# Turned quarters ahead of the scores, attention outputs later, and GpSimd normalising in two more units of a fused attention and gated-MLP kernel

## The chip, the cores and the metric

The kernel runs on one core of one Trainium2 chip. The metric is the device time of one execution in microseconds (us). Engines: PE (TensorE), with PEld for its weight loads, DVE (VectorE), ACT (ScalarE), POOL (GpSimd) and SP (SyncE), which here only issues DMAs.

## What is computed

Attention over 8 batches, 12 heads, 448 positions and 64 dimensions per head, with a softmax whose denominator has one extra term, and then two matrix products with an activation (Mish) between them:

```
scores = (q @ k.T) / sqrt(64)
m      = max(scores, axis=-1)
e      = exp(scores - m)
attn   = e / (sum(e) + exp(-m) + 1e-9)
x      = (attn @ v), heads side by side        # 3584 x 768
h      = x @ w_in                              # 3584 x 2048
out    = (h * tanh(softplus(h))) @ w_out       # 3584 x 768
```

Inputs and output are float32; the kernel's matrix products take bf16.

## The kernel before

Heads are taken in pairs: six pairs a batch, 48 in all, numbered from 0. The scores of a pair need seven tiles of 128 query rows, done in four half steps of two, two, two and one tiles. There are three pairs of score banks (`sc`), used in turn, and two single banks (`mo`) for everything else.

For a half step PE writes the scores, DVE takes the negated row maximum (L270, `negm`), and ACT writes the exponentials with their sums (L283) into one of four buffers `en`, chosen by the pair's number modulo four. So pair 10 overwrites pair 6's buffer and pair 11 overwrites pair 7's. Once a pair is done, its exponentials are multiplied by the reciprocal denominators (`normalise`, L302: seven passes of 128x448, on DVE at L317, or on GpSimd at L315, with a copy of the reciprocals made by DVE at L308), and then turned so that keys lie on partitions (`eT`). Most pairs are turned by a DMA transpose that SP issues (L321). Pairs 5, 6 and 7 (`BY_PE`) are turned by PE instead, a quarter at a time: `turn_on_pe` makes seven transposes into an `mo` bank (L332) and DVE copies the bank out (L336). `av_pair` (L344) multiplies a pair's `eT` with v (L358) and the result is copied into `xT` (L367).

Pairs 0 to 5 are done in a loop of their own. After it the work goes in units of three pairs; unit 2 holds pairs 6 to 8 and unit 3 pairs 9 to 11. A unit has twelve half steps (loop over n, L546), followed by eight blocks of the first matrix product and Mish (loop over f, `mm1_mish`, L375). The product in units 2 and 3 is that of batch 0, so it needs pairs 0 to 5 alone. From unit 4 on the half steps also carry parts of the second matrix product (L446), dealt out by weight.

The order is written by hand. Within a half step it is: the exponentials, the outstanding bank copies (`flush_late`), parts of the second product, the scores of the half step three ahead as far as score banks are free, loads and casts, attention outputs (`AV_AT`), turned quarters, and weight loads (`W_AT`). Each engine runs its instructions in the order in which the program issues them. Casts to bf16 and normalising share GpSimd with the issue of the weight loads (L148). Loads of q, k and v and the DMA transposes share SP's queue.

In the f loop of a unit, its first pair in the order `todo` is normalised at f = 0, the second at f = 3, and the third at f = 4 on GpSimd from unit 4 on, or at f = 7 on DVE in units 2 and 3. `todo` puts pairs turned by PE last: 8, 6, 7 in unit 2 and 9, 10, 11 in unit 3.

Of the kernel before, what the change touches and what calls it, by code (L numbers as in the profile page):

```python
# [15 lines left out]
UNIT_PAIRS = 3  # L16
# [3 lines left out]
def kernel(  # L20
# [15 lines left out]
    NT = 4  # L36
# [5 lines left out]
    UNITS_PER_B = HP // UNIT_PAIRS  # L42
    N_UNITS = B * UNITS_PER_B
    HU = 2 * UNIT_PAIRS
    FF_U = FF_T // UNITS_PER_B
# [3 lines left out]
    STEPS = 4  # L49
# [53 lines left out]
    def flush_late():  # L103
        while late:
            late.popleft()()

    def mo_take():

        if not mo_free:
            flush_late()  # L110
        return mo_free.popleft()
# [183 lines left out]
    def denominators(st):  # L295
        nc.vector.scalar_tensor_tensor(
            out=st["den"], in0=st["sums"], scalar=1e-9, in1=st["expm"],
            op0=ALU.add, op1=ALU.add,
        )
        nc.vector.reciprocal(out=st["rden"], in_=st["den"])  # L300

    def normalise(p, dma=True, on_pool=False):  # L302
        st = att[p]
        en = st["en"]
        if on_pool:

            st["rden2"] = st_pool.tile([128, NTILE], FP32, tag="rden2", name="rden2")
            nc.vector.tensor_copy(out=st["rden2"], in_=st["rden"])  # L308
        for i in range(NTILE):
            args = dict(  # L310
                out=en[:, :, i, 0:SP_], in0=en[:, :, i, 0:SP_],
                scalar1=st["rden2" if on_pool else "rden"][:, i : i + 1],
            )
            if on_pool:
                nc.gpsimd.tensor_scalar(scalar2=1.0, op0=ALU.mult, op1=ALU.mult, **args)  # L315
            else:
                nc.vector.tensor_scalar(scalar2=None, op0=ALU.mult, **args)  # L317
        eT = eT_pool.tile([128, NT, 2 * S], BF16, tag="eT", name="eT")
        st["eT"] = eT
        if dma:  # L320
            nc.sync.dma_start_transpose(  # L321
                out=eT.rearrange("c j (i q) -> c (j i) q", q=128),
                in_=en.rearrange("q j i c -> q (j i c)"),
            )

    def turn_on_pe(p, j, act=False):

        st = att[p]
        own = mo_take()
        ps = own[:, :].bitcast(BF16).rearrange("c (i q) -> c i q", q=128)  # L330
        for i in range(NTILE):
            nc.tensor.transpose(ps[0:SP_, i, :], st["en"][:, j, i, 0:SP_], ident)  # L332
        copy = nc.scalar.copy if act else nc.vector.tensor_copy

        def evac():
            copy(  # L336
                out=st["eT"][0:SP_, j, :].rearrange("c (i q) -> c i q", q=128),
                in_=ps[0:SP_, 0:NTILE, :],
            )
            mo_free.append(own)  # L340

        late.append(evac)
# [74 lines left out]
    def mm2_part(g, i, q0, nq):  # L417

        b0, b1 = 2 * g, 2 * g + 1
        cols, n_cols = slice(q0 * NQ, (q0 + nq) * NQ), nq * NQ  # L420
        st = {}
        if i < 3:
            src, c0 = gT[b0], i * 128
        elif i == 3:
            src, c0 = mids[g], 0
        else:
            src, c0 = gT[b1], i * 128 - S

        def evac():
            if (g, i) not in o_sbs:  # L430
                o_sbs[g, i] = [o_pool.tile([128, d_model], FP32, tag="o_sb", name="o_sb"), 0]
            o_sb, have = o_sbs[g, i]
            nc.vector.tensor_copy(out=o_sb[:, cols], in_=st["o"][:, 0:n_cols])  # L433
            mo_free.append(st["o"])
            o_sbs[g, i][1] = have + nq
            if (g, i) == (B // 2 - 1, 6):
                store_rows(g, i, o_sb, cols)
            elif have + nq == 4:
                store_rows(g, i, o_sb, slice(0, d_model))

        def chunk(f0, f1):
            if f0 == 0:
                flush_late()
                st["o"] = mo_take()
            for ff in range(f0, f1):
                nc.tensor.matmul(  # L446
                    st["o"][:, 0:n_cols],
                    lhsT=src[:, ff, c0 : c0 + 128],
                    rhs=w_out_sb[:, ff, cols],
                    start=(ff == 0), stop=(ff == FF_T - 1),  # L450
                )
            if f1 == FF_T:
                late.append(evac)

        step = 2
        return [(lambda f0=f0: chunk(f0, f0 + step), nq) for f0 in range(0, FF_T, step)]

    steps = UNIT_PAIRS * STEPS
    first_mm2 = 2 * UNITS_PER_B
# [27 lines left out]
    LOAD_AT = (0, 3, 6)  # L487
    HEAD = HP

    BY_PE = {HEAD - 1: 1, HEAD: 0, HEAD + 1: STEPS}  # L490
    AV_AT = {0: {5: 3, 7: 4, 10: 5}, 1: {3: 8, 6: 6, 10: 7}}

    W_AT = ({5: 1, 9: 1}, {1: 1, 5: 1, 7: 1, 9: 1, 11: 1}, {1: 1, 3: 1, 5: 1, 7: 1})
    for p in range(UNIT_PAIRS):
        load_pair(p)
    for p in range(2):
# [35 lines left out]
    denominators(att[HEAD - 1])  # L532
    normalise(HEAD - 1, dma=HEAD - 1 not in BY_PE)

    for u in range(UNITS_PER_B, N_UNITS + 2 * UNITS_PER_B):
        attn = u < N_UNITS
        filler = deque()
        for part in plan.get(u, []):
            filler.extend(mm2_part(*part))
        total, done, acc = sum(w for _, w in filler), 0, 0.0  # L540
        p0 = u * UNIT_PAIRS
        if attn and u >= first_mm2:
            av_with.update({p0 + i: p0 + i - UNIT_PAIRS for i in range(UNIT_PAIRS)})
        end = min((u + 1) * UNIT_PAIRS, N_PAIRS) * STEPS

        for n in range(steps):  # L546
            pi, s = divmod(n, STEPS)
            p, idx = p0 + pi, p0 * STEPS + n
            late_tp = u == UNITS_PER_B and n == STEPS
            if late_tp:  # L550
                transpose_pair(p0 + 2)
            exps(idx)
            if late_tp:
                evac_qk(p0 + 2)
            if u == UNITS_PER_B + 1 and n == 0:
                for j in range(2):
                    turn_on_pe(HEAD, j)
            flush_late()
            acc += weight[n]
            want = int(total * acc / sum(weight) + 1e-6)  # L560
            while done < want:
                fn, w = filler.popleft()
                fn()
                done += w
            scores_ahead(end)
            if n in LOAD_AT:
                load_pair(p0 + LOAD_AT.index(n) + LEAD)
                cast_pair(p0 + LOAD_AT.index(n) + LEAD - 1)
            early = AV_AT.get(u - UNITS_PER_B)
            if early is not None:  # L570
                if n in early:
                    av_pair(early[n])
                for pe, n0 in BY_PE.items():
                    first = 2 if pe == HEAD else 0
                    if pe // UNIT_PAIRS == u - 1 and n0 + first <= n < n0 + NT:
                        turn_on_pe(pe, n - n0)
            elif s == (2 if pi else 0) and N_PAIRS <= p < N_PAIRS + UNIT_PAIRS:
                av_pair(p - UNIT_PAIRS)
            if u - UNITS_PER_B < len(W_AT):
                load_w(W_AT[u - UNITS_PER_B].get(n, 0))  # L580
        assert done == total

        moe = u < N_UNITS + UNITS_PER_B
        b, w = (u - UNITS_PER_B) // UNITS_PER_B, u % UNITS_PER_B
        nxt = p0 + UNIT_PAIRS
        todo = sorted(range(p0, nxt), key=lambda p: p in BY_PE)
        for f in range(FF_U):
            if moe:
                mm1_mish(b, w * FF_U + f)
            if u == UNITS_PER_B and f in (2, 6) or u == UNITS_PER_B + 1 and f == 1:  # L590
                load_w(1)
            if not attn:
                continue
            if f == 0:
                denominators(att[p0]["whole"])
                normalise(todo[0], dma=todo[0] not in BY_PE)
            if f == 3:
                scores_ahead(min(nxt * STEPS + 1, N_PAIRS * STEPS))
            if f in (1, 3, 5):
                transpose_pair(nxt + f // 2, bank=f // 2 % 2)  # L600
                evac_qk(nxt + f // 2)
            if f >= FF_U - 2:
                scores_ahead(min(nxt * STEPS + f - FF_U + 4, N_PAIRS * STEPS))
            if f == 3:
                normalise(todo[1], dma=todo[1] not in BY_PE)
            if f == (4 if u >= first_mm2 else FF_U - 1):
                normalise(todo[2], dma=todo[2] not in BY_PE, on_pool=u >= first_mm2)
        if moe and w == UNITS_PER_B - 1:
            gather_mid(b)
    flush_late()  # L610
# [31 lines left out]
```

## Time and profile before

| | |
|---|---|
| time, median of 3 runs | 493.58 us (492.65 to 493.93) |
| time of the profiled execution | 492.95 us |
| its span | 491.2 us |
| PE busy | 451.8 us (92%) |
| DVE busy | 352.7 us (72%) |
| ACT busy | 349.5 us (71%) |
| POOL busy | 152.1 us (31%) |
| PE's share of the chain that ended last | 74% |

Times in the views are counted in us from the start of the span. A slice is one fortieth of the span, 12.28 us, and its digit the busy share in tenths. `[2.07 <-ACT en L283]` behind an instruction says how long its engine stood idle before it, and what released it. A view of waits gives the total, the number and the longest of the waits of one kind. `x7` says that seven instructions are merged into one row. The rows of a table by stretches have, after the length, the busy time of PE, PEld, DVE, ACT and POOL with the number of instructions, then the granted PE clock (1.00 is full), the mean busy share of the DMA engines, and GB/s.

### The profile page before, as it was taken

How to read it: one execution, taken by the hardware profiler on the slowest of the kernel's cores; microseconds unless marked ns; L12 is line 12 of the kernel's file. 1: busy time of each engine (PE TensorE's matmuls, PEld its weight loads, DVE VectorE, ACT ScalarE, POOL GpSimd, SP SyncE). 2: the span in 40 equal slices, each digit the busy share in tenths (PEclk: the TensorE clock that was granted, in tenths of full speed). 3: DMA queues.
4: the chain of work that ended last, by engine and by line, in shares of the span. 5: the costliest groups of instructions: out<-in, count | busy, mean ns of one | idle time of the engine just before them, and what ended most of it. 6: DMA issues, size and time to landing. Idle time of an engine off the chain costs nothing.

```text
span 491.2 us, 8805 instructions
## 1 busy us (share of the span) xinstructions
PE 451.8 (92%) x2992; PEld 249.3 (51%) x2992; DVE 352.7 (72%) x714; ACT 349.5 (71%) x906; POOL 152.1 (31%) x252
## 2 busy tenths in 40 slices
PE   4466995898999999999999999999999999999996
PEld 2222442454555555555555555556555565556563
DVE  4898987788868787878788786878797878420021
ACT  5988675768788887979697978888797979502300
POOL 4622270701433534252523324253435230300000
PEclk9999998799999999999999999999999999999999
DMA  8999999999999999899999979898999796780112
GB/s 221 207 211 214 245 212 154 239 166 223 190 231 249 215 226 195 240 187 250 147 247 198 216 175 206 209 216 234 176 260 174 170 177 141 132 157 21 45 37 93
DMA packets 209452, 92.19 MB, mean 188 GB/s; under 512 B 166272, under 2 KB 205952, under 8 KB 209408
## 3 DMA queue, kind: packets, MB, share of 16 engines
q1 hardware_dynamic: 201920, 85.35, 81.7%
q0 software_dynamic: 7488, 6.29, 9.1%
q8 instruction: 23, 0.38, 0.3%
q14 instruction: 21, 0.17, 0.1%
HBM read 45.61 MB, written 11.01 MB: 115 GB/s over the span
## 4 chain that ended last, share of the span: by engine, by line
PE 74%; DVE 10%; ACT 7%; DMA 6%; issue 2%; SPq 1%; POOL 0%; DVEq 0%; ACTq 0%
PE mo L446 26%; PE mo L382 24%; PE sc L249 9%; ACT en L283 6%; PE sc L358 6%; DVE negm L270 5%; DMA eT<-en 5%; PE sc L382 3%; DVE en L317 3%; PE sc L179 3%; PE mo L358 1%; DMA k_f<-in_k_dram 1%; DVE xT L367 1%; SPq L121 1%; PE mo L332 0%
## 5 line engine op out<-in xcount | busy, mean ns | idle before, releaser
L283 ACT ACTIVATE en<-sc,negm 128x448 bf16<-128x448 f32 x336 | 209.6, 638 | 31.9 <-DVE negm L270 14.5
L270 DVE TENSOR_REDUCE negm<-sc 128x2 f32<-128x896 f32 x192 | 182.6, 969 | 56.3 <-PE sc L249 44.9
L446 PE MATMUL mo<-w_out_sb,gT 128*128 128x384 bf16 (+1 forms) x896 | 142.1, 303 | 0.0
L382 PE MATMUL mo<-xT,w_in_sb 128*128 128x448 bf16 x672 | 140.3, 352 | 0.4 <-DVE xT L367 0.4
L388 ACT ACTIVATE gT<-mo 128x448 bf16<-128x448 f32 x112 | 59.4, 543 | 72.4 <-PE mo L382 72.2
L446 PEld LDWEIGHTS <-gT 128*128 128x128 bf16 x896 | 84.0, 98 | 46.8 <-issue 1.3
L382 PEld LDWEIGHTS <-w_in_sb 128*128 128x128 bf16 x768 | 72.8, 98 | 64.6 <-issue 3.8
L315 POOL TENSOR_SCALAR en<-en,rden 128x448 bf16<-128x448 bf16 x84 | 52.8, 650 | 93.8 <-DVE rden L308 86.9
L162 POOL CAST q_bf<-q_f 112x512 bf16<-112x512 f32 x47 | 28.9, 616 | 160.2 <-DMA q_f<-in_q_dram 151.1
L249 PE MATMUL sc<-kT,qd 128*128 128x448 bf16 x252 | 71.6, 354 | 1.5 <-DVE qd L210 0.7
L317 DVE TENSOR_SCALAR en<-en,rden 128x448 bf16<-128x448 bf16 x252 | 69.7, 347 | 0.9
L283 ACT ACTIVATION_READ_ACCUMULATOR en<-sc,negm 128x1 f32 x336 | 69.4, 207 | 0.0
L433 DVE COPY o_sb<-mo 128x384 f32<-128x384 f32 (+1 forms) x64 | 32.1, 502 | 41.3 <-PE mo L446 41.2
L249 PEld LDWEIGHTS <-qd 128*128 128x128 bf16 x252 | 23.9, 97 | 31.8 <-issue 13.8
L358 PE MATMUL sc<-eT,v_bf 112*64 112x448 bf16 x288 | 34.1, 357 | 2.0 <-ACT en L283 1.8
L164 POOL CAST v_bf<-v_f 112x512 bf16<-112x512 f32 x48 | 29.6, 616 | 15.4 <-DMA v_f<-in_v_dram 14.1
L255 PE MATMUL sc<-kT,qd 64*128 64x448 bf16 x36 | 17.7, 508 | 17.9 <-ACT en L283 16.1
L358 PEld LDWEIGHTS <-v_bf 112*64 112x64 bf16 x384 | 21.0, 115 | 25.4 <-issue 18.7
L163 POOL CAST k_bf<-k_f 112x512 bf16<-112x512 f32 x47 | 29.0, 617 | 5.1 <-DMA k_f<-in_k_dram 4.0
L210 DVE TENSOR_SCALAR qd<-sc 64x448 bf16<-64x448 bf16 x72 | 27.8, 386 | 0.9
L218 ACT COPY kT<-sc 128x448 bf16<-128x448 bf16 x39 | 20.8, 534 | 7.0 <-PE sc L179 7.0
L446 PE MATMUL mo<-w_out_sb,mid 128*128 128x384 bf16 x128 | 24.9, 326 | 0.0
(50 smaller groups left out, 307.3 us busy)
## 6 DMA issues: line engine op xcount, KB each, us to landing
q_f<-in_q_dram SPq DMA_DIRECT2D x48, 224.0 KB, 5.1
k_f<-in_k_dram SPq DMA_DIRECT2D x48, 224.0 KB, 5.3
v_f<-in_v_dram SPq DMA_DIRECT2D x48, 224.0 KB, 5.5
w_in_sb<-in_moe_w_in_dram POOLq DMA_DIRECT2D x12, 256.0 KB, 5.8
w_out_sb<-in_moe_w_out_dram POOLq DMA_DIRECT2D x8, 384.0 KB, 7.5
out_dram<-o_sb SPq DMA_DIRECT2D x7, 336.0 KB, 3.4
out_dram<-o_sb SPq DMA_DIRECT2D x8, 288.0 KB, 4.5
out_dram<-o_sb SPq DMA_DIRECT2D x8, 240.0 KB, 3.4
```

The costliest lines, as they stand in the source:

```text
L163: cast_k(out=k_bf, in_=k_f.rearrange(by_t, t=NT))
L164: nc.gpsimd.tensor_copy(out=v_bf, in_=v_f)
L249: nc.tensor.matmul(sc[:, bk, 0:S], lhsT=qT[:, i].rearrange("d h r -> d (h r)"), rhs=kT, start=True, stop=True,)
L270: nc.vector.tensor_reduce(out=negm, in_=sc[:, 0 : len(cols), 0:S], axis=AX.X, op=ALU.max, negate=True)
L283: nc.scalar.activation(out=st["en"][:, :, c, 0:SP_], in_=sc[:, bk, 0:S].rearrange("q (j c) -> q j c", j=NT), func=AF.Exp, bias=st["negm"][ ...
L315: nc.gpsimd.tensor_scalar(scalar2=1.0, op0=ALU.mult, op1=ALU.mult, **args)
L317: nc.vector.tensor_scalar(scalar2=None, op0=ALU.mult, **args)
L358: nc.tensor.matmul(av[h * 64 : (h + 1) * 64, 0:S], lhsT=v_bf[:, h, j * D : (j + 1) * D], rhs=e_h, start=(j == 0), stop=(j == NT - 1),)
L382: nc.tensor.matmul(h_ps[:, 0:S], lhsT=w_in_sb[:, dm, ff * 128 : (ff + 1) * 128], rhs=xT[b][:, dm, :], start=(dm == 0), stop=(dm == DM_T - 1),)
L388: nc.scalar.activation(out=gT[b][:, ff, :], in_=h_ps[:, 0:S], func=AF.Mish)
L433: nc.vector.tensor_copy(out=o_sb[:, cols], in_=st["o"][:, 0:n_cols])
L446: nc.tensor.matmul(st["o"][:, 0:n_cols], lhsT=src[:, ff, c0 : c0 + 128], rhs=w_out_sb[:, ff, cols], start=(ff == 0), stop=(ff == FF_T - 1),)
```

## The change

In unit 3 the quarters of pairs 6 and 7 are turned ahead of the scores and of the bank copies of their half step, so that each copy follows in the same half step. Before, the first two of pair 6 stood so, and the others stood at the end of half steps 2 to 7, behind the attention outputs. Now they are at half steps 0 (two), 1 and 2 for pair 6 and 3 to 6 for pair 7. The attention outputs of pairs 8, 6 and 7, which stood at half steps 3, 6 and 10, become those of 6, 7 and 8 at 5, 8 and 10. Pair 5's quarters in unit 2 stay where they are.

The third pair in `todo` is normalised at f = 4 on GpSimd in units 2 and 3 too. One weight load moves from the f loop of unit 3 into its half steps, and those of unit 4 stand two half steps later.

```diff
-    BY_PE = {HEAD - 1: 1, HEAD: 0, HEAD + 1: STEPS}
-    AV_AT = {0: {5: 3, 7: 4, 10: 5}, 1: {3: 8, 6: 6, 10: 7}}
-
-    W_AT = ({5: 1, 9: 1}, {1: 1, 5: 1, 7: 1, 9: 1, 11: 1}, {1: 1, 3: 1, 5: 1, 7: 1})
+    BY_PE = (HEAD - 1, HEAD, HEAD + 1)
+    TURN_AT = (
+        {1 + j: [(HEAD - 1, j)] for j in range(NT)},
+        {0: [(HEAD, 0), (HEAD, 1)], 1: [(HEAD, 2)], 2: [(HEAD, 3)],
+         3: [(HEAD + 1, 0)], 4: [(HEAD + 1, 1)], 5: [(HEAD + 1, 2)], 6: [(HEAD + 1, 3)]},
+    )
+    AV_AT = ({5: 3, 7: 4, 10: 5}, {5: 6, 8: 7, 10: 8})
+
+    W_AT = ({5: 1, 9: 1}, {1: 1, 4: 1, 5: 1, 7: 1, 9: 1, 11: 1}, {3: 1, 5: 1, 7: 1, 9: 1})
...
-            if u == UNITS_PER_B + 1 and n == 0:
-                for j in range(2):
-                    turn_on_pe(HEAD, j)
+            if u == UNITS_PER_B + 1:
+                for part in TURN_AT[1].get(n, []):
+                    turn_on_pe(*part)
             flush_late()
...
-            early = AV_AT.get(u - UNITS_PER_B)
-            if early is not None:
+            if u - UNITS_PER_B < len(AV_AT):
+                early = AV_AT[u - UNITS_PER_B]
                 if n in early:
                     av_pair(early[n])
-                for pe, n0 in BY_PE.items():
-                    first = 2 if pe == HEAD else 0
-                    if pe // UNIT_PAIRS == u - 1 and n0 + first <= n < n0 + NT:
-                        turn_on_pe(pe, n - n0)
+                if u == UNITS_PER_B:
+                    for part in TURN_AT[0].get(n, []):
+                        turn_on_pe(*part)
...
-            if u == UNITS_PER_B and f in (2, 6) or u == UNITS_PER_B + 1 and f == 1:
+            if u == UNITS_PER_B and f in (2, 6):
                 load_w(1)
...
-            if f == (4 if u >= first_mm2 else FF_U - 1):
-                normalise(todo[2], dma=todo[2] not in BY_PE, on_pool=u >= first_mm2)
+            if f == 4:
+                normalise(todo[2], dma=todo[2] not in BY_PE, on_pool=True)
```

## The prediction

> **What bounds the kernel now.** I read the page first (busy shares, slices, chain), then the chain in order of time, then the waits and the timelines of the unit that the diff edits (pairs 9 to 11, 76 to 98 us). First the page: span, busy times, the slices of PE and of its granted clock, and the chain by engine.
>
> ```profile
> span 491.2 us, 8805 instructions
> PE 451.8 (92%) x2992; PEld 249.3 (51%) x2992; DVE 352.7 (72%) x714; ACT 349.5 (71%) x906; POOL 152.1 (31%) x252
> ...
> PE   4466995898999999999999999999999999999996
> ...
> PEclk9999998799999999999999999999999999999999
> ...
> PE 74%; DVE 10%; ACT 7%; DMA 6%; issue 2%; SPq 1%; POOL 0%; DVEq 0%; ACTq 0%
> ```
>
> From slice 8 (98 us) on PE is full and is the chain. So a time saved before that slice moves everything after it forward, as long as nothing later is tied to another clock. Slices 6 and 7 (74 to 98 us) have PE at 5 and 8 and a lowered clock. The chain in order of time (start, length, work) says why:
>
> ```profile
> 69.55 15.42 DMA eT<-en
> 85.01 1.71 PE mo L358 x8
> ```
>
> The transpose of pair 8, started at 69.55, lands at 84.97; PE stands at pair 8's attention outputs until then. Behind them, in PE's order, is the last turned quarter of pair 6. Pair 10 writes its exponentials into pair 6's buffer (four buffers, p modulo 4), and so ACT waits for that quarter; pair 11 waits in the same way for pair 7's last quarter. The waits of 76 to 97 us, and ACT's timeline at both places:
>
> ```profile
> ACT en L283 <- PE mo L332: 7.6, 2, 5.1
> ...
> PE mo L358 <- DMA eT<-en: 1.9, 1, 1.9
> ```
> ```profile
> 77.50 0.63 ACT L283 ACTIVATE en<-sc,negm 128x448 bf16<-128x448 f32 x1
> ...
> 87.03 0.63 ACT L283 ACTIVATE en<-sc,negm 128x448 bf16<-128x448 f32 x1 [5.11 <-PE mo L332]
> ...
> 93.99 0.64 ACT L283 ACTIVATE en<-sc,negm 128x448 bf16<-128x448 f32 x1 [2.53 <-PE mo L332]
> ...
> 98.27 0.25 ACT L293 ACTIVATE expm<-negm 128x21 f32<-128x21 f32 x1
> ```
>
> ACT's 21 exponentials run from 77.50 to 98.27: 20.8 us, of which 5.11 + 2.53 = 7.6 us are waits. Without them it is 13.1 us, 0.61 us each.
>
> **The change, part by part.** The same instructions run on PE, DVE, ACT and SP, except that 14 normalising passes go from DVE to GpSimd; the rest is order.
>
> *The turns and the attention outputs.* Pair 6's quarters now stand at half steps 0, 0, 1, 2 and pair 7's at 3 to 6, each ahead of that half step's scores and evacuated at once; pair 8's outputs go from half step 3 to 10, pair 6's from 6 to 5, pair 7's from 10 to 8. So nothing in PE's order up to half step 10 waits for the DMA, and both ACT waits lose their cause. What is late next? For that I take DVE in its new order. Its rows (start, length), beside PE's at the lowered clock (88.94, 89.86, and 85.01 above) and at the full one (93.73, 95.69):
>
> ```profile
> 90.53 1.09 DVE L270 TENSOR_REDUCE negm<-sc 128x2 f32<-128x896 f32 x1
> 91.54 0.61 DVE L336 COPY eT<-mo 112x896 bf16<-112x896 bf16 x1
> 92.07 1.08 DVE L270 TENSOR_REDUCE negm<-sc 128x2 f32<-128x896 f32 x1
> 93.06 0.61 DVE L367 CAST xT<-mo 128x448 bf16<-128x448 f32 x1
> 93.60 0.61 DVE L336 COPY eT<-mo 112x896 bf16<-112x896 bf16 x1
> ...
> 95.86 0.62 DVE L270 TENSOR_REDUCE negm<-sc 128x1 f32<-128x448 f32 x1
> ```
> ```profile
> 78.89 0.35 PE L263 MATMUL sc<-kT,qd 64*64 64x448 bf16 x1 [2.07 <-ACT en L283]
> ...
> 88.94 0.99 PE L332 MATMUL mo<-ident,en 128*112 128x128 bf16 x7
> 89.86 0.55 PE L255 MATMUL sc<-kT,qd 64*128 64x448 bf16 x1
> ...
> 93.73 0.55 PE L332 MATMUL mo<-ident,en 128*112 128x128 bf16 x7
> ...
> 95.69 0.95 PE L358 MATMUL mo<-eT,v_bf 112*64 112x448 bf16 x8
> 96.56 2.44 PE L382 MATMUL mo<-xT,w_in_sb 128*128 128x448 bf16 x12
> ...
> 102.33 0.55 PE L249 MATMUL sc<-kT,qd 128*128 128x448 bf16 x2 [0.61 <-ACT gT L388]
> ```
>
> From start to start a two-bank reduce takes 1.01 us, a quarter's copy 0.53, an xT cast 0.54; a one-bank reduce I put at 0.54 (0.62 less the same overlap). Half step 3's scores still start at 78.89, since they wait for ACT's first bank, and DVE's reduce follows at about 79.3. From there to the end of half step 10's reduce DVE has six two-bank reduces (6.06), two one-bank ones (1.08), six quarter copies (3.18) and one cast (0.54): 10.9 us, so 90.2 at the earliest. Followed by hand through the three score banks, the handovers of 0.1 to 0.2 us leave some 0.7 us of gaps, so 90.9. ACT then has three exponentials (1.8 us) and ends at 92.7 to 92.9: 5.4 us sooner than 98.27. DVE, not a wait, now sets this stretch.
>
> PE: half step 8's reduce ends at about 87.1 (7.8 us after 79.3), its exponentials at 88.5, then come the last scores (89.0) and two blocks of attention outputs. At full clock (0.95 each) the gated matmuls start at 91.1, at the lowered one (1.71 each, with the turns at 0.99) at 92.7, against 96.56: 5.5 or 3.9 us sooner. In the next step the path from ACT's end over the denominators to the first scores of pair 12, where PE now waits 0.61 us, moves by ACT's 5.4: the slow case gets those 0.6 back (4.5), the fast case is held at 5.4. **I take 4.8**, nearer the slow one, since the clock is the one thing here that the order doesn't fix. Its rows (PE busy, granted clock after DVE, ACT and POOL):
>
> ```profile
> 76.00:80.00 4.00, 1.20 (x16) 0.98 (x16) 4.00 (x11) 3.97 (x11) 0.00 (x0) 1.00 1.40 81
> 80.00:84.00 4.00, 2.06 (x13) 1.13 (x13) 3.62 (x5) 1.93 (x7) 0.00 (x0) 0.72 1.30 149
> 84.00:88.00 4.00, 2.63 (x15) 1.56 (x15) 1.40 (x3) 0.96 (x3) 2.09 (x4) 0.50 1.12 321
> ```
>
> The granted clock is 1.00 while PE does 1.20 of 4 us, 0.72 in the next 4 and 0.50 after. The new order still leaves PE without work from 76.8 to 78.9 (the 2.07 us at 78.89) but then gives it a turn in every half step. Of the clock I take no more than the fast case's 5.4 as the upper bound and the slow case's 4.5 as the lower. The Trainium skill ("TensorE: Matmul & The Clock Gate", section "What's actually happening") has the clock halved after an idle window of about 3.4 us and restored after a busy one; by that rule the new stretch, whose longest gap is 2.1 us, would keep the full clock and gain 5.4 where I take 4.8. The row at 80 falls with PE busy 2.06 of 4 us, which is no idle window, so the trace bears the rule out only in part.
>
> *GpSimd's normalising.* Pair 7's seven passes leave DVE at 76.95 (1.81 us), pair 11's shortly ahead of 113.27; each leaves a short copy of the reciprocals on DVE.
>
> ```profile
> L315 POOL TENSOR_SCALAR en<-en,rden 128x448 bf16<-128x448 bf16 x84 | 52.8, 650 | 93.8 <-DVE rden L308 86.9
> ```
> ```profile
> 65.69 3.37 DVE L317 TENSOR_SCALAR en<-en,rden 128x448 bf16<-128x448 bf16 x7
> ...
> 71.11 1.90 DVE L317 TENSOR_SCALAR en<-en,rden 128x448 bf16<-128x448 bf16 x7
> ...
> 76.95 1.81 DVE L317 TENSOR_SCALAR en<-en,rden 128x448 bf16<-128x448 bf16 x7
> ...
> 105.41 1.81 DVE L317 TENSOR_SCALAR en<-en,rden 128x448 bf16<-128x448 bf16 x7
> ...
> 113.27 0.62 DVE L270 TENSOR_REDUCE negm<-sc 128x1 f32<-128x448 f32 x1 [0.50 <-PE sc L249]
> ```
> ```profile
> 67.18 2.14 POOL L148 DMA_DIRECT2D w_in_sb<-in_moe_w_in_dram  x3
> ...
> 90.08 2.99 POOL L148 DMA_DIRECT2D w_out_sb<-in_moe_w_out_dram  x4
> ```
>
> Neither is a gain of its own: ACT's start at 77.50 follows the last Mish, and after pair 11's passes DVE idles 0.5 us for PE's scores at 113.27. On GpSimd seven passes of 0.650 are 4.6 us. Pair 7's start when DVE has done pair 6 (71.11 and 1.90: about 73.0) and end at 77.6; the first turn of pair 7 is due at about 81.8, so 4 us spare. Pair 11's follow pair 10's on DVE (105.41 and 1.81, less 4.8: 102.4) and end at about 107, where DVE's own would end at about 107.6, and its transpose leaves no later than before. Beside a busy GpSimd a DVE normalise took 3.37 instead of 1.81 us (65.69), while the quarter copies beside GpSimd's casts (91.54) keep 0.61; so I charge nothing.
>
> *GpSimd's queue.* Behind pair 7's passes wait one piece of w_in (issued at about 68.6, now at about 77.6), pair 12's casts and another piece; pair 12's transposes and these pieces' matmuls come behind the start of the gated matmuls (91.1 at the earliest). The pieces of w_out keep their places after the casts of pairs 13 and 14. Their landing times and first use:
>
> ```profile
> DMA to landing us min/median/max: 5.1/7.5/8.9
> ```
> ```profile
> 109.02 2.44 PE L446 MATMUL mo<-w_out_sb,gT 128*128 128x384 bf16 x14
> ```
>
> The last of the first four is issued by 93.1 and lands by 102.0; it is used after 104.2 (109.0 less 4.8). At zero, covered by 2.2 us; beyond that each us late is one of PE's. SP's order is unchanged.
>
> **The sum.** The profiled execution took 492.95 us, 1.75 of them around the span, and is 0.63 under the median of 493.58. Less 4.8: 488.15 by it, 488.8 by the median. I say 488.5.
>
> **The rivals.**
> *Full clock throughout (chance 0.20).* PE never falls below DVE's pace, the stretch is set by DVE and ACT alone, and 5.4 us go: 487.6 by the profiled execution, 488.2 by the median; 487.9. For it: a turn in each half step. Against: the row at 80.
>
> *Half the gain (0.18).* Two banks hold turns and outputs, and each copy now stands between two reduces. If that costs each of the seven half steps 3 to 9 another 0.4 us over DVE's 1.54 (1.01 + 0.53), 2.8 of the 4.8 us go: 491.3. For it: at the lowered clock turn and scores are 0.99 + 0.55 = 1.54 as well, so two engines with no room to spare hand to each other. Against: each has three score banks' worth of lead.
>
> *No change (0.06).* The DMA shares above (1.40, 1.30, 1.12) show full queues; what moves up could wait for its loads instead, at 493.2. Against: PE has one wait for a DMA in this unit, and the chain's time from 98 us on is PE's.
>
> *Slower (0.08).* GpSimd ends pair 7 so late that the turns, the scores behind them and ACT stand as they now do for the DMA. Each us beyond 81.8 costs one, and from 86.6 the gain is gone: 13.6 us for seven passes, 1.94 each in place of 0.650. At 2.4 each they would end at 89.8, 3.2 us further: 496.5. For it: operations of DVE and GpSimd do stretch beside each other (3.37 over 1.81). Against: that stretch would make 8.5 us of the 4.6, ending at 81.5, just in time.
>
> *The forecast*, 4.0 to 5.2 us less, has 0.48.
>
> **How the numbers follow.** 0.3% (1.5 us) is about what a measurement of this kernel can tell from no change. The forecast, the full clock and half the gain lie below that: 0.86 faster; same 0.06, slower 0.08. The forecast's own range is 488.0 to 489.6. The range for 8 in 10 reaches down to a DVE without gaps (90.2, so 0.7 us beyond the full clock: 487.0) and up to the half gain (491.3); no change and slower are left out, with the worse part of the half gain.
>
> **What would show it.** In the changed kernel's profile: ACT's waits for turned quarters in this unit under 1.5 us in all (7.6 now); no PE wait for eT there; the unit's gated matmuls starting near 92 instead of 96.56; DVE nearly without idle time from 79 to 91; GpSimd's first normalise near 73, with seven passes under 5 us. Right for the wrong reason would be a clock that stays at 1.0 with DVE idle. Wrong would be a PE wait for POOL at the turns of pair 7, or a new wait for w_out or a cast between 98 and 130 us.

## The result and the profile after

The changed kernel takes 489.79 us (median of 16 runs, 487.49 to 494.88), the kernel before 493.69 in the same comparison (491.89 to 495.67): a ratio of 0.9924, with a 95% interval of 0.9904 to 0.9943. That is 3.9 us less by the medians and 2.8 to 4.7 by the interval.

The profiled execution took 492.75 us, with a span of 491.0; 14 of the 16 runs were shorter. To see where its time went I cut both traces at ACT's table loads, which stand at the two ends of each unit's half steps: L283 loads the exponential's table when the half steps begin, L388 that of Mish when the f loop begins. Before, and then after (start, length):

```profile
65.11 1.28 ACT L388 ACT_TABLE_LOAD   x1
76.21 1.28 ACT L283 ACT_TABLE_LOAD   x1
98.54 1.28 ACT L388 ACT_TABLE_LOAD   x1
109.23 1.28 ACT L283 ACT_TABLE_LOAD   x1
125.70 1.28 ACT L388 ACT_TABLE_LOAD   x1
135.97 1.28 ACT L283 ACT_TABLE_LOAD   x1
152.26 1.28 ACT L388 ACT_TABLE_LOAD   x1
```
```profile
66.89 1.28 ACT L388 ACT_TABLE_LOAD   x1
78.36 1.28 ACT L283 ACT_TABLE_LOAD   x1
95.09 1.28 ACT L388 ACT_TABLE_LOAD   x1
105.78 1.28 ACT L283 ACT_TABLE_LOAD   x1
122.25 1.28 ACT L388 ACT_TABLE_LOAD   x1
132.69 1.28 ACT L283 ACT_TABLE_LOAD   x1
150.92 1.28 ACT L388 ACT_TABLE_LOAD   x1
```

The half steps of unit 3 take 95.09 - 78.36 = 16.73 us in place of 98.54 - 76.21 = 22.33: 5.6 us less. Its f loop (10.69) and the half steps of unit 4 (16.47) are the same to the hundredth. But this execution came to unit 2's f loop 1.8 us later, ahead of anything that the change touches, and the half steps of unit 5 take 18.23 us where they took 16.29. The first the change can't have caused: the fourteen profiles of this document, whose order is the same up to there, come to that loop between 65.11 and 67.11 us, the kernel before first of all. The second is in every trace below that has the new places of the weight loads.

In unit 3 ACT's waits of 76 to 97 us no longer have a turned quarter among them:

```profile
ACT gT L388 <- PE mo L382: 1.6, 2, 1.0
ACT en L283 <- DVE negm L270: 0.8, 2, 0.6
ACT en L283 <- PE sc L258: 0.7, 1, 0.7
```

DVE runs on end there (its groups from 79.1 to 92.3: busy time, mean ns | idle before), with 1.9 us idle, 1.3 of it ahead of half step 3's reduce:

```profile
L270 DVE TENSOR_REDUCE negm<-sc 128x2 f32<-128x896 f32 (+1 forms) x9 | 8.8, 982 | 1.9 <-PE sc L266 1.3 <-PE sc L258 0.6
L336 DVE COPY eT<-mo 112x896 bf16<-112x896 bf16 x8 | 4.8, 615 | 0.0
L367 DVE CAST xT<-mo 128x448 bf16<-128x448 f32 x1 | 0.6, 615 | 0.0
```

What is new stands in unit 5. The chain, and PE's wait of 126 to 150 us:

```profile
125.13 12.44 DMA eT<-en
```
```profile
PE sc L358 <- DMA eT<-en: 1.9, 1, 1.9
```

The transpose of pair 12 takes 12.4 us to land, where it took 9.4, and PE waits for it with pair 12's attention outputs. Ahead of it GpSimd has issued four loads of w_out, 384 KB each:

```profile
118.94 1.55 POOL L148 DMA_DIRECT2D w_out_sb<-in_moe_w_out_dram  x2
...
122.51 1.48 POOL L148 DMA_DIRECT2D w_out_sb<-in_moe_w_out_dram  x2
```

Before, there were three, as one had gone out at 94.71, and pair 12's transpose started at 128.41 (its own line last):

```profile
122.89 1.48 POOL L148 DMA_DIRECT2D w_out_sb<-in_moe_w_out_dram  x2
...
126.03 0.74 POOL L148 DMA_DIRECT2D w_out_sb<-in_moe_w_out_dram  x1
```
```profile
DMA to landing us min/median/max: 9.4/9.4/9.4
```

Unit 5's f loop is longer too, 11.40 us for 10.22. At its start DVE normalises pair 15; before, these passes stood alone, and now they run beside pair 20's casts (before, after, and the first of the casts after):

```profile
152.82 1.81 DVE L317 TENSOR_SCALAR en<-en,rden 128x448 bf16<-128x448 bf16 x7
```
```profile
151.78 2.92 DVE L317 TENSOR_SCALAR en<-en,rden 128x448 bf16<-128x448 bf16 x7
```
```profile
152.27 0.62 POOL L162 CAST q_bf<-q_f 112x512 bf16<-112x512 f32 x1 [0.88 <-DMA q_f<-in_q_dram]
```

### The profile page after: what moved, and what is told of

It is laid out like the page before. It is cut to its first block, busy times and chain, and to the rows that moved or that the text cites. A ratio compares the mean times of both kernels' runs of the same rounds, so it can differ in the third digit from the quotient of the medians.

```text
span 491.0 us, 8804 instructions
## 1 busy us (share of the span) xinstructions
PE 450.5 (92%) x2992; PEld 248.5 (51%) x2992; DVE 351.3 (72%) x702; ACT 350.2 (71%) x906; POOL 161.5 (33%) x266
## 4 chain that ended last, share of the span: by engine, by line
PE 68%; DVE 14%; ACT 9%; DMA 4%; issue 2%; SPq 1%; POOL 0%; DVEq 0%; ACTq 0%
PE mo L446 24%; PE mo L382 23%; PE sc L249 8%; ACT en L283 8%; DVE negm L270 7%; PE sc L358 6%; DVE en L317 4%; PE sc L382 3%; PE sc L179 3%; DMA eT<-en 3%; DMA k_f<-in_k_dram 1%; PE mo L358 1%; PE sc L255 1%; DVE xT L367 1%; DVE eT L336 1%
## 5 line engine op out<-in xcount | busy, mean ns | idle before, releaser
L283 ACT ACTIVATE en<-sc,negm 128x448 bf16<-128x448 f32 x336 | 209.7, 637 | 28.7 <-DVE negm L270 16.3
L388 ACT ACTIVATE gT<-mo 128x448 bf16<-128x448 f32 x112 | 59.4, 543 | 73.5 <-PE mo L382 73.3
L315 POOL TENSOR_SCALAR en<-en,rden 128x448 bf16<-128x448 bf16 x98 | 61.7, 649 | 115.8 <-DVE rden L308 106.0
L283 ACT ACTIVATION_READ_ACCUMULATOR en<-sc,negm 128x1 f32 x336 | 69.2, 206 | 0.0
L317 DVE TENSOR_SCALAR en<-en,rden 128x448 bf16<-128x448 bf16 x238 | 67.2, 354 | 0.9
```

Of the source, the lines that this page charges most:

```text
L283: nc.scalar.activation(out=st["en"][:, :, c, 0:SP_], in_=sc[:, bk, 0:S].rearrange("q (j c) -> q j c", j=NT), func=AF.Exp, bias=st["negm"][ ...
L388: nc.scalar.activation(out=gT[b][:, ff, :], in_=h_ps[:, 0:S], func=AF.Mish)
```

## The experiments

The theory to start with (A): the order gives 5.5 us, GpSimd's part nothing, and the new places of the weight loads take about 1.5 back in unit 5. Twelve runs were made, of ten new kernels and two again. The stages below come from the profiles, cut as above; "U3 half" is unit 3's half steps, "U3 f" its f loop, and so on, in us.

| kernel | time, median | ratio to before (95%) | profiled run | U2 f | U3 half | U3 f | U4 half | U4 f | U5 half |
|---|---|---|---|---|---|---|---|---|---|
| before | 493.69 | | 492.95 | 11.10 | 22.33 | 10.69 | 16.47 | 10.27 | 16.29 |
| changed | 489.79 | 0.9924 (0.9904 to 0.9943) | 492.75 | 11.47 | 16.73 | 10.69 | 16.47 | 10.44 | 18.23 |
| changed, again | 490.62 | 0.9921 (0.9895 to 0.9947) | 490.89 | 10.94 | 16.76 | 10.70 | 16.46 | 10.65 | 17.84 |
| changed, old weight places | 489.59 | 0.9904 (0.9883 to 0.9925) | 489.12 | 11.00 | 16.77 | 10.69 | 16.47 | 11.10 | 16.29 |
| the same, again | 489.94 | 0.9915 (0.9882 to 0.9948) | 489.88 | 11.03 | 16.94 | 10.70 | 16.45 | 11.38 | 16.29 |
| changed, DVE normalises | 492.78 | 0.9966 (0.9942 to 0.9990) | 495.18 | 11.84 | 16.74 | 12.77 | 16.47 | 11.00 | 19.90 |
| order alone | 493.72 | 0.9971 (0.9942 to 1.0001) | 493.82 | 10.71 | 16.75 | 12.30 | 20.66 | 10.66 | 16.38 |
| changed, no loads late in unit 4 | 493.92 | 0.9980 (0.9957 to 1.0004) | 496.38 | 11.17 | 16.74 | 11.51 | 22.63 | 11.18 | 16.29 |
| GpSimd alone | 493.14 | 0.9977 (0.9955 to 0.9999) | 492.85 | 10.91 | 21.03 | 10.69 | 16.47 | 11.03 | 16.29 |
| before, two loads later | 494.52 | 1.0008 (0.9973 to 1.0043) | 497.27 | 14.42 | 20.85 | 10.69 | 16.46 | 10.86 | 16.29 |
| changed, GpSimd for pair 7 only | 490.90 | 0.9927 (0.9898 to 0.9956) | 490.14 | 11.29 | 16.55 | 10.70 | 16.46 | 10.39 | 17.72 |
| changed, GpSimd for pair 11 only | 492.85 | 0.9976 (0.9948 to 1.0003) | 493.02 | 12.45 | 16.95 | 10.70 | 16.46 | 10.25 | 17.96 |
| weight places alone | 495.74 | 1.0019 (0.9996 to 1.0041) | 496.42 | 10.66 | 23.75 | 10.69 | 16.47 | 10.51 | 17.29 |
| changed, two loads earlier | 490.83 | 0.9933 (0.9909 to 0.9958) | 489.77 | 11.21 | 16.74 | 11.51 | 17.46 | 11.00 | 16.29 |

The medians come from several sessions, so kernels are best compared by their ratios. The stages are those of one execution each, the "profiled run"; for the changed kernel and in experiments 2, 4 and 7 it is 2.4 to 3.0 us longer than the median.

**1. The weight loads back in their old places.**

```diff
-    W_AT = ({5: 1, 9: 1}, {1: 1, 4: 1, 5: 1, 7: 1, 9: 1, 11: 1}, {3: 1, 5: 1, 7: 1, 9: 1})
+    W_AT = ({5: 1, 9: 1}, {1: 1, 5: 1, 7: 1, 9: 1, 11: 1}, {1: 1, 3: 1, 5: 1, 7: 1})
...
-            if u == UNITS_PER_B and f in (2, 6):
+            if u == UNITS_PER_B and f in (2, 6) or u == UNITS_PER_B + 1 and f == 1:
```

> The changed kernel with the weight loads where the kernel before has them (one at f = 1 of unit 3, unit 4's four at half steps 1, 3, 5, 7). Theory A: the order of turns and outputs brings about 5.5 us in unit 3, and the changed place of unit 4's loads gives part of it back in unit 5, because the transpose of pair 12 starts behind four of them (12.4 us to landing, PE waits 1.9 us). Then this kernel is 1 to 2 us faster than the changed one's 489.8: 488 to 489, with pair 12's transpose landing in under 10 us and no PE wait for it. Theory B: the loads' place does not matter, and what was lost was a late start: 489.8, within 0.7 us of the changed kernel.

Measured 489.59 and, when it was run again (experiment 5), 489.94. One of the four loads now goes out ahead of the crowd (108.89), three after 119:

```profile
108.89 0.81 POOL L148 DMA_DIRECT2D w_out_sb<-in_moe_w_out_dram  x1
119.47 1.48 POOL L148 DMA_DIRECT2D w_out_sb<-in_moe_w_out_dram  x2
122.61 0.80 POOL L148 DMA_DIRECT2D w_out_sb<-in_moe_w_out_dram  x1
```

Pair 12's transpose lands in 9.1 us, PE waits for no transpose, and unit 5's half steps take 16.29 us again: in the stage theory A holds. In the whole time it doesn't clear the noise, and 489.59 is what theory B gave; unit 4's f loop takes 0.7 us longer.

**2. DVE normalises the third pair again.**

```diff
-            if f == 4:
-                normalise(todo[2], dma=todo[2] not in BY_PE, on_pool=True)
+            if f == (4 if u >= first_mm2 else FF_U - 1):
+                normalise(todo[2], dma=todo[2] not in BY_PE, on_pool=u >= first_mm2)
```

> The changed kernel with the third pair of units 2 and 3 normalised on DVE at f = 7, as before. Theory A: GpSimd's part is worth nothing by itself (before, DVE idled or ACT started no earlier): 489.8, within 0.7 us of the changed kernel, and ACT's 21 exponentials of unit 3 within 0.5 us of 15.2 us. Theory B: the earlier normalising, not the order, is what lets the turns go ahead: 1.8 us and more is lost, 491.6 or later, with ACT's exponentials taking 17 us or more.

Measured 492.78. Theory A is right on the stage and wrong on the time, theory B the other way round: unit 3's half steps take 16.74 us, so the turns go ahead as well without GpSimd, and yet 2 to 3 us of the gain are gone. Two of them are in unit 3's f loop (12.77 for 10.69). Its normalising of pair 9 on DVE, GpSimd's work at that time, and PE's waits of 93 to 103 us:

```profile
95.03 3.89 DVE L317 TENSOR_SCALAR en<-en,rden 128x448 bf16<-128x448 bf16 x7
```
```profile
94.49 2.23 POOL L148 DMA_DIRECT2D w_out_sb<-in_moe_w_out_dram  x3
96.69 0.64 POOL L162 CAST q_bf<-q_f 112x512 bf16<-112x512 f32 x1
97.25 0.70 POOL L163 CAST k_bf<-k_f 112x512 bf16<-112x512 f32 x1
97.90 0.65 POOL L164 CAST v_bf<-v_f 112x512 bf16<-112x512 f32 x1
```
```profile
PE sc L249 <- DVE qd L210: 2.0, 1, 2.0
```

In the changed kernel the same seven passes take 1.81 us, with GpSimd idle since 91.6:

```profile
95.64 1.81 DVE L317 TENSOR_SCALAR en<-en,rden 128x448 bf16<-128x448 bf16 x7
```

Here they run beside three load issues and pair 15's casts and take 3.89; the copy of pair 12's queries stands behind them on DVE, and PE waits 2.0 us for it. The Trainium skill ("SBUF — State Buffer", section "Who interferes with whom") has VectorE's two-port operations and GpSimd's hold a shared port pair in turn, each blocking the other for a whole instruction; the 2.08 us by which DVE's passes stretch agree.

This profile also has 19.90 us in unit 5's half steps: PE waits 1.9 us there for pair 12's transpose, and from 141.2 to 144.6 its granted clock is 0.50.

**3. The order alone** (edits 1 and 2 together).

> The kernel before with the new places of turns and attention outputs alone. Theory A: the whole gain, and none given back in unit 5: 488 to 489, that is 4.5 to 5.5 us below the kernel before, ACT's exponentials of unit 3 in 15 to 16 us in place of 20.8. Theory B: under half of that, 491.5 or later, as the turns of pair 7 wait for DVE's normalising.

Measured 493.72. Unit 3's half steps are right (16.75), and everything is given back: pair 9's passes take 3.37 us (unit 3's f loop 12.30), and pair 9's transpose, started at 97.15 behind five loads, lands after 14.0 us:

```profile
97.15 13.97 DMA eT<-en
```
```profile
PE sc L358 <- DMA eT<-en: 3.5, 1, 3.5
```

Unit 4's half steps take 20.66 us for 16.47. So the order brings its 5.6 us and, alone, hardly any time: whatever starts sooner meets GpSimd's and the DMA's work, which did not move.

**4. No loads behind pair 16's casts.**

```diff
-    W_AT = ({5: 1, 9: 1}, {1: 1, 4: 1, 5: 1, 7: 1, 9: 1, 11: 1}, {3: 1, 5: 1, 7: 1, 9: 1})
+    W_AT = ({5: 1, 9: 1}, {1: 1, 4: 1, 5: 1, 7: 2, 9: 2, 11: 1}, {1: 2})
```

> The changed kernel with two of unit 4's four loads moved up into half steps 7 and 9 of unit 3 and the other two to half step 1 of unit 4, so that none is issued after pair 16's casts. Theory A: pair 12's transpose finds only the loads of q, k and v ahead of it and lands in 6 to 8 us, with no PE wait; 1.5 to 2.5 us faster than the changed kernel: 487.3 to 488.3. Theory B: 489.8, within 0.7 us. A third way: the loads now meet the transposes of pairs 9 to 11, which then land over 9 us after their start, and PE waits for one of them in unit 4: 490 or later.

Measured 493.92, the third way. Two loads go out at 110.30, just as pair 11's transpose starts, and it lands after 13.8 us:

```profile
110.26 13.76 DMA eT<-en
```
```profile
PE sc L358 <- DMA eT<-en: 6.1, 2, 5.6
```

**5. Changed kernel and old weight places on one chip.** No new edits.

> The changed kernel itself, beside the others on one chip. Both theories: 489.8 within 1 us, ACT's stage of unit 3 (from its table load to the next) 16.7 us. It is the yardstick for the kernel with the old places of the weight loads: theory A has it 1 us slower than that one, theory B level with it.

> The changed kernel with the old places of the weight loads, again, on the same chip as the changed kernel. Theory A (four loads ahead of pair 12's transpose cost PE a wait of up to 1.9 us, and three or fewer don't): 1 us or more faster than the changed kernel and no PE wait for a transpose. Theory B (no effect): within 0.5 us of it.

Measured 490.62 and 489.94, ratios 0.9921 and 0.9915. The new weight places cost unit 5's half steps 1.55 us here (17.84 for 16.29), while unit 4's f loop is 0.7 us shorter with them. By the time the two can't be told apart, so theory A's "1 us or more" isn't shown. In this second profile of the changed kernel pair 12's transpose takes 12.0 us, but PE's wait at its outputs (1.5 us) is put down to ACT, while the weight load ahead of it waits 1.9 us for the transpose.

**6. GpSimd's part alone, on the kernel before** (edit 2 the other way round).

> The kernel before with GpSimd normalising the third pair at f = 4 in units 2 and 3, and nothing else. Theory C: GpSimd's seven passes hold back the weight loads behind them in its queue, so that pair 8's transpose lands in 9 us in place of 15.4 and PE no longer waits 1.95 us for it; the turns still stand behind the attention outputs, so only those 2 us go: ACT's stage of unit 3 takes 20 to 21 us in place of 22.3 and the kernel 491 to 492.5. Theory D: the DMA was the whole of ACT's 7.6 us of waits, and the order itself brings nothing: 488 to 489.5. Theory E: GpSimd's part has nothing to do with the transpose: 493.7, no change.

Measured 493.14 (0.9977). Pair 8's transpose lands in 8.2 us in place of 15.4, PE's wait for it is gone, and unit 3's half steps take 21.03 us: theory C in the stage, a little less than it said in the time. ACT still waits 6.3 us for turned quarters:

```profile
ACT en L283 <- PE mo L332: 6.3, 2, 3.4
```

So in the old order landing the transpose in time is worth 1.3 us of the stage, and the new order brings 4.3 more. In the new order the landing is worth nothing there: in experiments 2, 3 and 9 it takes 15.0, 14.9 and 13.5 us, and the stage is as short as in the others. Theory D falls.

**7. Two of the loads ahead of pair 8's transpose issued later, on the kernel before.**

```diff
-    W_AT = ({5: 1, 9: 1}, {1: 1, 5: 1, 7: 1, 9: 1, 11: 1}, {1: 1, 3: 1, 5: 1, 7: 1})
+    W_AT = ({5: 1, 9: 1}, {4: 3, 7: 1, 9: 1, 11: 1}, {1: 1, 3: 1, 5: 1, 7: 1})
...
-            if u == UNITS_PER_B and f in (2, 6) or u == UNITS_PER_B + 1 and f == 1:
+            if u == UNITS_PER_B and f == 2 or u == UNITS_PER_B + 1 and f == 1:
```

> The kernel before with two of the five w_in loads ahead of pair 8's transpose issued later (behind pair 13's casts), and nothing else. Theory C: as with GpSimd alone, pair 8's transpose lands in about 9 us, PE's wait of 1.95 us goes, ACT's stage of unit 3 takes 20 to 21 us, and the kernel 491 to 492.5. Theory D: 488 to 489.5. Theory E: the loads do not slow the transpose, which lands in 15 us as before: 493.7.

The transpose lands in 7.1 us and unit 3's half steps take 20.85, as theory C says; theory E falls. But the time is 494.52, no gain: without the third load issue ahead of them pair 12's casts come 0.7 us sooner in the unit (69.81 - 66.25 = 3.56 in place of 69.32 - 65.11 = 4.21), beside pair 8's passes on DVE, which take 4.29 us, and PE waits for the copy behind them:

```profile
67.62 4.29 DVE L317 TENSOR_SCALAR en<-en,rden 128x448 bf16<-128x448 bf16 x7
```
```profile
PE sc L255 <- DVE qd L200: 2.6, 1, 2.6
```

Unit 2's f loop takes 14.42 us, the longest of all.

**8 and 9. GpSimd for one of the two pairs only.**

```diff
-            if f == 4:
-                normalise(todo[2], dma=todo[2] not in BY_PE, on_pool=True)
+            if f == (FF_U - 1 if u == 3 else 4):     # the other kernel: u == 2
+                normalise(todo[2], dma=todo[2] not in BY_PE, on_pool=u != 3)
```

> The changed kernel with only pair 7 normalised on GpSimd; pair 11 goes back to DVE at f = 7. Theory F: what GpSimd's part brings is the order in its own queue around pair 7. With those passes ahead of the weight loads, pair 8's transpose lands in about 9 us, the loads of pairs 13 to 15 start 6 us sooner, and casts and weight loads are over before DVE normalises pair 9 near 94.5. So pair 9's normalise takes 1.8 us, the f loop of unit 3 (ACT's table load to the next) 10.7, and the kernel is within 0.7 us of the changed one (489.8 to 490.6). Theory G: it is pair 11's passes that hold back the casts of pair 15 and keep them off pair 9's normalise: pair 9 takes over 3 us, the f loop 12 us or more, and the kernel 492 or more.

> The changed kernel with only pair 11 normalised on GpSimd; pair 7 goes back to DVE at f = 7 of unit 2. Theory F: pair 8's transpose is issued in over 12 us again, the loads and casts of pairs 13 and 14 come late, and three w_out loads meet pair 9's normalise: it takes 2.5 us or more, the f loop of unit 3 11.3 us or more, and the kernel 491 to 492.8. Theory G: pair 15's casts are out of the way, and that is all there is to it: 1.8 us for pair 9, 10.7 for the f loop, 490 for the kernel.

With pair 7 alone the kernel takes 490.90 (0.9927), level with the changed one: pair 8's transpose 8.7 us, pair 9's passes 1.81, unit 3's f loop 10.70. With pair 11 alone it takes 492.85 (0.9976). So by the time pair 7's passes carry nearly all of GpSimd's part, as theory F says. In the second kernel F's path is wrong, though: pair 9's passes take 1.81 us and unit 3's f loop 10.70, as theory G says, because pair 15's casts are out of the way. Its profile shows 1.0 to 1.5 us more in unit 2's f loop (12.45) than the two of the changed kernel, with a wait of 1.7 us for the queries' copy there, and it came to that loop 0.2 to 0.7 us later, where the order is the same. But the other kernels with pair 7 on DVE have 10.66 to 11.84 in that loop (14.42 in experiment 7), so this is no regular loss. What makes pair 7's passes worth their time by themselves is not shown.

**10. The weight places alone, on the kernel before** (edit 1 the other way round).

> The kernel before with the new places of the weight loads alone. Theory A: unit 3 is unchanged (22.3 us for ACT's stage), and in unit 5 the transpose of pair 12 starts behind four loads in place of three and PE waits for it 1 to 2 us: 494.5 to 496. Theory B: no effect, 493.7 to 494.1.

Measured 495.74, ratio 1.0019 (0.9996 to 1.0041): not told from no change. Pair 12's transpose takes 11.3 us, PE waits 0.8 for it, and unit 5's half steps take 17.29: theory A in this stage. Unit 3's half steps, which it had unchanged, take 23.75 us in this profile, with 9.1 us of ACT's waits for turned quarters in place of 7.6; why stays open.

**11. Two loads earlier, one late.**

```diff
-    W_AT = ({5: 1, 9: 1}, {1: 1, 4: 1, 5: 1, 7: 1, 9: 1, 11: 1}, {3: 1, 5: 1, 7: 1, 9: 1})
+    W_AT = ({5: 1, 9: 1}, {1: 1, 4: 1, 5: 1, 7: 2, 9: 1, 11: 2}, {1: 1, 3: 1})
```

> The changed kernel with eight loads in unit 3 (two more, at half steps 7 and 11) and two in unit 4, at half steps 1 and 3. Theory A: one load stands ahead of pair 12's transpose and one beside pair 11's; neither makes PE wait, and DVE's normalising of pair 12 is free of a load issue beside it, so that unit 4's f loop takes 10.3 to 10.6 us and unit 5's half steps 16.3: 1 to 2 us faster than the changed kernel, 488.3 to 489.3. Rival: the eight loads of unit 3 delay the transposes of pairs 9 to 11 so that PE waits in unit 4, whose half steps take 17 us or more: 490 or later.

Measured 490.83 (0.9933), level with the changed kernel. Unit 5 is free (16.29, transpose in 7.0 us), but unit 4's half steps take 17.46 with a wait of 1.5 us for a transpose, and unit 3's f loop 11.51: partly the one, partly the rival. Of all that was run, the changed kernel with the old weight places has the lowest ratio, within the noise of the changed one.

The time to landing of a transpose, over all fourteen profiles, beside the loads that GpSimd issues in the 8 us ahead of it:

| transpose | loads ahead | landing, us |
|---|---|---|
| pair 12 (384 KB each) | 0 or 1 | 7.8, 7.0 |
| pair 12 | 3 | 8.9, 8.9, 9.1, 9.3, 9.4, 10.6 |
| pair 12 | 4 | 11.3, 11.9, 12.0, 12.2, 12.4, 12.4 |
| pair 8 (256 KB each) | 3 | 7.1 to 9.0 in nine profiles |
| pair 8 | 5, one or two of them up to 3 us behind its start | 13.5, 14.9, 15.0, 15.4, 15.7 |
| pair 9 | 0 or 1 | 6.1 to 6.4 in four profiles |
| pair 9 (384 KB each) | 2 or 3 | 6.5 to 7.2 in six profiles, 11.3 and 11.8 in two |
| pair 9 | 5, for the 9.6 one of them of 256 KB | 9.6, 14.0 |

For pairs 12 and 8 it goes with the count. For pair 9 the count of these 8 us is not enough: the 11.3 and 11.8 are those of experiments 11 and 4, where five loads went out in a row from 9.5 us ahead. Loads just behind a transpose's start count as well: pair 11's lands after 9.3 to 10.1 us with one (experiments 1, 5 and 11) and after 13.8 with two (experiment 4), against 6.1 with none (the changed kernel). No run here separates the number from the distance.

## Why the prediction was right, and where it was not

It said 488.5 (487.0 to 491.3) and faster; the median is 489.79, inside that range and 0.2 us above its narrow one (488.0 to 489.6). By its own steps:

*The turns and outputs.* The forecast had ACT's 21 exponentials end 5.4 us sooner. Counted from the first to the end they take 94.83 - 79.66 = 15.17 us in place of 20.77: 5.6. DVE sets the stretch, as it said: its reduce of half step 3 starts 1.9 us after ACT's first exponential (79.3 less 77.50 had made 1.8), and the gated matmuls start 14.2 us after it (93.84 less 79.66), where 91.1 to 92.7 less 77.50 had made 13.6 to 15.2. In all ten profiles with the changed order, whatever stood beside it, that stage takes 16.55 to 16.95 us. That it was the order and not the DMA's lateness is shown by experiments 6 and 7: landing the transpose in time is worth 1.3 to 1.5 us of the stage in the old order, and by experiments 2, 3 and 9 nothing in the new one.

*The clock.* It was split into two cases of 4.5 and 5.4 us, and 4.8 taken between. PE's longest gap in this stretch of the changed kernel, and its rows of 80 to 92 us (granted clock third from the end):

```profile
81.05 0.35 PE L263 MATMUL sc<-kT,qd 64*64 64x448 bf16 x1 [2.07 <-ACT en L283]
```
```profile
80.00:84.00 4.00, 2.62 (x20) 1.65 (x19) 2.48 (x5) 4.00 (x14) 3.96 (x7) 0.79 1.05 235
84.00:88.00 4.00, 3.71 (x33) 2.46 (x33) 4.00 (x7) 3.65 (x12) 2.85 (x5) 0.78 1.11 272
88.00:92.00 4.00, 2.46 (x27) 1.35 (x23) 4.00 (x7) 2.65 (x9) 3.20 (x5) 1.00 1.20 245
```

The clock falls and is back at 88. In the second profile of the same kernel it is 0.59 and 0.55 in the first two rows, and the stage takes 16.76 us for 16.73. In the profiles of experiments 2 and 8 it is 1.00 throughout the stretch, and the stage takes 16.74 and 16.55. So the clock made at most 0.2 us of difference here, and the forecast's slow case had no ground. The Trainium skill's rule ("TensorE: Matmul & The Clock Gate", section "What's actually happening") would have kept the full clock, as PE's longest gap was the one at 81.05; the clock fell all the same. All that PE did from 77.99 to 81.05 was pair 6's first two turns (0.99 us).

*GpSimd's normalising, put at zero.* This step failed. It said that neither pair's passes are a gain of their own because DVE or ACT had slack at that place. Experiment 2 puts their worth at 2 to 3 us, and 8 nearly all of it on pair 7. What was missed is that the passes move GpSimd's other work. Beside experiment 2, the loads behind them start later, pair 8's transpose is through SP in 5.9 to 6.8 us in place of 12.6, the loads of pairs 13 to 15 follow 6 to 8 us sooner in the unit, and GpSimd's casts and issues are over before pair 9 is normalised on DVE. That is worth 2.1 us in unit 3's f loop. It is not all that pair 7's passes do: in experiment 9, without them, pair 9's passes take 1.81 us as well, and yet the ratio is 0.5% worse than in 8. That cause stays open. The row that says what a meeting costs, 3.37 us in place of 1.81, was quoted, but only asked what GpSimd's new passes would meet. With unit 3's half steps 5 us shorter, pair 9's normalising would have moved onto the casts and load issues that stood at 93 to 95 us. That the sum came out right on this point is luck: the change has both parts.

*GpSimd's queue, put at zero, "covered by 2.2 us".* The loads were checked against their own users, and PE waits for none of these from 94 to 150 us. They were not checked against the transposes that share the DMA. Four loads of unit 4 ahead of pair 12's transpose cost unit 5's half steps 1.55 to 1.94 us in the two profiles. This is the term that took part of the 5.6 us back in these stages: the forecast's 4.8 was too small in unit 3 by 0.8 and too large in unit 5 by up to 1.9, and by 0.9 to 1.2 more in unit 5's f loop. So the nearness of 4.8 to the measured 3.9 is in part two errors that offset each other. From the start of unit 2's f loop to the end of unit 5's the two profiles are 1.9 and 2.9 us shorter than the one before; the measured 3.9 (2.8 to 4.7) is more, and where the rest lies is not shown. The prediction's sign for this term, a wait for w_out or a cast between 98 and 130 us, could not show it: PE's new wait is for a transpose and ends at 137.61. The rival "no change" named the DMA, but for PE's loads in general and with the argument that the chain from 98 us on is PE's; that argument said nothing of a kernel whose chain moves.

*The rivals.* "Slower" needed pair 7 late by 4 us; its passes ran from 75.34 and took 4.33 us, so they ended 4.5 us ahead of pair 7's first turn at 84.17. "Half the gain" needed 0.4 us a half step of handovers, and DVE's idle time after half step 3's reduce was 0.6 us at most.

## What to carry to other kernels

Ask of a stretch that starts sooner not only what it waits for, but what it will now run beside: here 5.6 us won in one stage were lost again (experiment 3) to a DVE stage and a transpose that moved onto work of GpSimd and the DMA that stayed. A transfer has two prices, its own deadline and the delay of the transfer behind it that something waits for, and an instruction inserted into a queue that also issues DMAs moves all that is behind it. Where a change has several parts, look for the one that makes room for the others: it may look free and bring little alone (experiment 6: 0.23% of the 0.76%) and yet be needed.

## What the runs showed of the hardware

A DMA transpose that mostly lands in 6.1 to 7.2 us with no load or one near it took 8.9 to 10.6 (pair 12) with three loads of 384 KB issued by GpSimd in the 8 us ahead of it, 11.3 to 12.4 with four, and 13.5 to 15.7 (pair 8) with five of 256 KB, the last one or two just behind its start. Pair 9's shows that the count alone is not the rule (6.5 to 11.8 us with two or three). Seven DVE passes of 128x448 in bf16 took 1.8 us alone and up to 4.3 beside GpSimd's casts and DMA issues, while reduces and copies out of score and turn banks beside the same work kept their 1.09 and 0.61 us. A halved PE clock for 3 to 7 us cost nothing that these runs can tell where DVE set the pace.
